# v as the stationary side of the packed values in a fused attention and two-layer-block kernel

## The chip, the core and the metric

The kernel runs on one core of a Trainium2 chip. Its engines are TensorE (PE; its weight loads are shown apart, as PEld), VectorE (DVE), ScalarE (ACT), GpSimd (POOL) and SyncE (SP). The metric is the device time of one execution in microseconds.

## The reference

An attention with 8 batches, 8 heads, 576 positions and head dimension 64 goes through 32 packed queries per head; its output then passes two blocks of matrix products. Cut to what matters here:

```python
def sm_attn(qq, kk, vv):
    s = scale * np.matmul(qq, kk.transpose(0, 1, 3, 2))
    s = s - np.max(s, axis=-1, keepdims=True)
    a = np.exp(s)
    a = a / (np.sum(a, axis=-1, keepdims=True) + 1e-09)
    return np.matmul(a, vv)
p_packed = sm_attn(p, k, v)              # 32 x 64 per head
out = sm_attn(q, p_packed, p_packed)     # 576 x 64 per head
x = out as (4608, 512)
h = ((x @ w1) * (x @ w2)) @ w3 @ w_out
h = g(h @ w_in) @ w_out2                 # g: a piecewise quadratic
```

The change is in the first of the two attentions, in `a / sum` and the product with v.

## The kernel before, in words

The program has three stages: the attention with the first block (to about 546 us), the second block's first product (to about 900 us) and its second. The change lies in the first.

A batch of the first stage is a list of 24 units on PE: 16 `ab_unit`s (L388: two products of 6 matmuls at L398, 128x288 each, multiplied with each other) and then 8 `x2_unit`s (L436: 24 matmuls at L422 through `x2_product`). While the units of batch b run, the attention of batch b+1 is made between them, one step behind a unit: the main loop (L748) puts step `spread[u]` behind unit u. A step has a part for PE and one for the other engines (`ew`); `emit` (L362) issues the first, then the second, and every engine and every DMA queue takes its instructions in the order in which they are issued. The steps of `attention` (L197), for batches 1 to 7 with `joint` set, are:

- `scores_k(G)` (L201), for half G of the heads: 8 matmuls of float32 (L190, through `eight`), DVE's maximum `mx` and `nb`, and ACT's exponential (L217) into a tile `e`, with the row sums into `c["sum"]`. For batch b+2 it stands behind units 20 and 22 of batch b.
- `turn_e(0)` and `turn_e(1)` behind unit 4: 10 transposes of `e` on PE (L234) and ACT's copies into `et` (L242). `turn_e(1)` also makes `rd`, the reciprocal of both halves' sums, on DVE (L248, L249).
- `packed` behind unit 8: 40 matmuls (L260) with `et` as the loaded side (32 columns, one head) and v as the moving side (64 columns); then DVE multiplies with `rd` into `pp` (L268).
- `turn_packed` behind unit 10: PE transposes `pp` (L277), ACT copies the result to `ppt` (L281), and SP loads the next batch's v and pb.
- `scores_q` behind unit 12, `normalise` and `split_a`: the second attention, from `ppt`.
- `build_m` behind units 20 and 22: matmuls of `ppt` with w1 and w2 (L190), split on ACT and DVE at L111 and L112.

Batch 0 and the steps of batch 1 are laid out by hand (`STEPS`, L51, and `TAIL`, L54): b0 and b1 are batch 1's `scores_k`, b4 its `packed`, b5 its `turn_packed`, k0 and k1 batch 2's `scores_k`, y0 to y7 the last `x2_unit`s of batch 0, whose results DVE adds to `xp` (L452), n0 to n3 batch 1's `build_m`, b9 a `normalise`, t1 a `split_a`. The tail ends

```python
'n1', 'n0', 'k0', 'y3', 'b9', 'y4', 'n3', 'n2', 'k1', 'y5', 't1', 'y6', 'y7'
```

In PSUM six banks k0 to k5 go round for the units (`psa`, L96): an `ab_unit` takes two, an `x2_unit` one. A tile of two banks, `psm`, serves the attention steps. Between the units DVE, ACT and the queues also prepare the second block's weights (`weight_tasks`, L628: raw, cvt, cvx, hl), one or two tasks a unit.

Of the kernel before, what the change touches and what calls it, by code (L numbers as in the profile page):

```python
# [8 lines left out]
F32 = mybir.dt.float32  # L9
# [4 lines left out]
AF = mybir.ActivationFunctionType  # L14
# [8 lines left out]
P = 128  # L23
HS = S // 2
NCH = 5
# [37 lines left out]
def fused_kernel(ctx: ExitStack, tc, qT, kT, vv, pb, w1, w2, w3T, wo, win, wout, out):  # L63
# [133 lines left out]
    def attention(b, joint=False):  # L197

        c = {}

        def scores_k(G):  # L201
            def pe():
                heads = loaded["k", b].rearrange("p a (r n) -> p (a r) n", r=2)
                c["ps"] = psm()
                eight([c["ps"][:, r, :HS] for r in range(2)], loaded["p", b][:, G],
                      lambda q: heads[:, 4 * G + q])

            def ew():
                mx = small(1, "mx")
                nc.vector.tensor_reduce(out=mx, in_=c["ps"][:, :, :HS], axis=AX.XY, op=ALU.max)  # L210
                nb = small(1, "nb")
                nc.vector.tensor_scalar(out=nb, in0=mx, scalar1=-SCALE, scalar2=None, op0=ALU.mult)
                if G == 0:
                    c["sum"] = small(2, "sum")
                    c["e"] = []
                e = big()
                nc.scalar.activation(  # L217
                    out=e.rearrange("p (a n) -> p a n", a=2), in_=c["ps"][:, :, :HS], func=AF.Exp,
                    scale=SCALE, bias=nb, accum_out=c["sum"][:, G:G + 1],
                )  # L220
                c["e"].append(e)
                if G == 1:
                    load_q(b)
            return pe, ew

        def turn_e(i):
            def pe():
                if i == 0:
                    c["et"] = a2.tile([CH, 2, NCH, P], F32, name="et", tag="et", bufs=1)
                alone = i and (joint or b == 0)  # L230
                ps = c["turn", i] = psa().rearrange("p (g n) -> p g n", g=2) if alone else psm()
                for G in range(2):
                    for x, ch in enumerate(TURNS[i]):
                        nc.tensor.transpose(  # L234
                            ps[:CHS[ch], G, x * P:(x + 1) * P],
                            c["e"][G][:, ch * CH:ch * CH + CHS[ch]], ident,
                        )

            def ew():
                chs = TURNS[i]  # L240
                rows = min(CHS[ch] for ch in chs)
                nc.scalar.activation(  # L242
                    out=c["et"][:rows, :, chs[0]:chs[-1] + 1, :].rearrange("p g c n -> p g (c n)"),
                    in_=c["turn", i][:rows, :, :len(chs) * P], func=AF.Copy,
                )
                if i == 1:
                    rd = small(2, "rd")
                    nc.vector.tensor_scalar(out=rd, in0=c["sum"], scalar1=1e-9, scalar2=None, op0=ALU.add)  # L248
                    nc.vector.reciprocal(out=rd, in_=rd)  # L249
                    c["rd"] = rd  # L250
            return pe, ew

        def packed():
            def pe():
                c["ps"] = psm()
                for G in range(2):
                    for ch in range(NCH):
                        for q in range(4):
                            h = 2 * q + G
                            nc.tensor.matmul(  # L260
                                c["ps"][32 * q:32 * q + 32, G, :D],
                                c["et"][:CHS[ch], G, ch, 32 * q:32 * q + 32],
                                loaded["v", b][:CHS[ch], ch, h * D:(h + 1) * D],
                                start=(ch == 0), stop=(ch == NCH - 1),
                            )

            def ew():
                nc.vector.tensor_tensor(  # L268
                    out=pp.rearrange("p (r d) -> p r d", r=2), in0=c["ps"][:, :, :D],
                    in1=c["rd"].unsqueeze(2).to_broadcast([P, 2, D]), op=ALU.mult,  # L270
                )
            return pe, ew

        def turn_packed():
            def pe():
                c["ps"] = psm()
                nc.tensor.transpose(c["ps"][:, 0, :P], pp, ident)  # L277

            def ew():
                c["ppt"] = a2.tile([P, P], F32, name="ppt", tag="ppt", bufs=1)  # L280
                nc.scalar.activation(out=c["ppt"], in_=c["ps"][:, 0, :P], func=AF.Copy)  # L281
                if 0 < b < B - 1:
                    load_v(b + 1)
                    load_p(b + 1)
            return pe, ew

        def scores_q(hf):
            def product(x):
                qt = loaded["q", b]
                ps = None if joint and x == 0 else psm()  # L290
                c["ps", x] = [ps[:, r] if ps is not None else psa() for r in range(2)]
                eight([p[:, :HS] for p in c["ps", x]], c["ppt"], lambda q: qt[:, q, x * HS:(x + 1) * HS])

            def pe():
                for x in ((hf,), (0, 1), ())[joint * (1 + hf)]:
                    product(x)

            def ew():
                l = big()
                for r in range(2):  # L300
                    nc.vector.transpose(out=l[:, r * HS:(r + 1) * HS], in_=c["ps", hf][r][:, :HS])
                l3 = l.rearrange("p (c n) -> p c n", n=NP)
                mx = small(S // NP, "qmx")
                nc.vector.tensor_reduce(out=mx, in_=l3, axis=AX.X, op=ALU.max)
                nc.vector.tensor_tensor(
                    out=l3, in0=l3, in1=mx.unsqueeze(2).to_broadcast([P, S // NP, NP]), op=ALU.subtract)
                c["l", hf] = l
                exp = lambda: nc.scalar.activation(out=l, in_=l, func=AF.Exp, scale=SCALE)
                if b:
                    exp()  # L310
                else:
                    later.append(exp)
                if hf == 1 and 0 < b < B - 1:
                    load_k(b + 1)
            return pe, ew

        def normalise(hf):
            def ew():
                l3 = c["l", hf].rearrange("p (c n) -> p c n", n=NP)
                sm = small(S // NP, "qsm")  # L320
                nc.vector.tensor_reduce(out=sm, in_=l3, axis=AX.X, op=ALU.add)
                nc.vector.tensor_scalar(out=sm, in0=sm, scalar1=1e-9, scalar2=None, op0=ALU.add)
                nc.vector.reciprocal(out=sm, in_=sm)
                nc.vector.tensor_tensor(
                    out=l3, in0=l3, in1=sm.unsqueeze(2).to_broadcast([P, S // NP, NP]), op=ALU.mult)
                t = big()
                nc.vector.transpose(out=t, in_=c["l", hf])
                c["t", hf] = t
            return None, ew

        def split_a(hf):
            def ew():
                if hf == 0:
                    at_tile[b] = a1.tile([P, 2, 2, S], F32R, name="at", tag="at", bufs=1)
                at = at_tile[b][:, :, :, hf * HS:(hf + 1) * HS]
                t = c["t", hf].rearrange("p (r n) -> p r n", r=2)
                nc.scalar.activation(out=at[:, :, 0], in_=t, func=AF.Copy)
                nc.vector.tensor_tensor(out=at[:, :, 1], in0=t, in1=at[:, :, 0].bitcast(F32), op=ALU.subtract)
            return None, ew

        def build_m(w, n):
            ps = []

            def pe():
                ps.extend([psa(), psa()])
                eight(ps, c["ppt"], lambda q: w12[w][n][:, q, :])

            def ew():
                m = a1.tile([P, 2, 2, 512], F32R, name=f"m{w}{n}", tag=f"m{w}{n}", bufs=1)
                for G in range(2):  # L350
                    split(m[:, :, G], ps[G])
                m_tile[b, w, n] = m
            return pe, ew

        return (
            [scores_k(0), scores_k(1), turn_e(0), turn_e(1), packed(), turn_packed(),
             scores_q(0), scores_q(1), normalise(0), normalise(1)],
            [split_a(0), split_a(1)],
            {(w, n): build_m(w, n) for w in range(2) for n in range(2)},
        )  # L360
# [931 lines left out]
```

## Time and profile before

| | us |
|---|---|
| median of 3 runs | 1247.66 |
| lowest and highest of them | 1245.33, 1247.72 |
| the profiled execution's own time | 1245.62 |
| its span | 1243.8 |
| PE busy | 1234.9 (99%) |
| DVE busy | 841.6 (68%) |
| ACT busy | 694.9 (56%) |

The span is what the profiler saw from the first to the last instruction. A float32 matmul stands in the trace as two MATMUL and two LDWEIGHTS records; a matmul of the type fp32r and a transpose stand there as one of each. Starts are measured, the ends of PE's records are modelled, so what a stretch costs is read from starts.

### The profile page before, as it was taken

To read this page: it belongs to the slowest core of one execution; us is meant where nothing else is said; L and a number is where in the kernel's file an instruction comes from. 1 tells how busy PE (TensorE), PEld (TensorE's weight loads), DVE (VectorE), ACT (ScalarE), POOL (GpSimd) and SP (SyncE) were. 2 spreads that over 40 slices of the span, in tenths; PEclk is the share of its full clock that TensorE was granted. 3 is DMA by queue.
4 is the path that set the end of the run, shared out by engine and by line. 5 is a ranking of instruction groups with operands and counts; after the bars stand their busy time and mean duration, and the time that the engine had idled before them with its cause. 6 is when DMAs were issued, how large, how long until landed. Compare 5 with 4: busy or idle time off the path is not lost.

```text
span 1243.8 us, 21614 instructions
## 1 busy us (share of the span) xinstructions
PE 1234.9 (99%) x8344; PEld 1100.6 (88%) x8344; DVE 841.6 (68%) x1358; ACT 694.9 (56%) x1184; POOL 47.1 (4%) x86
## 2 busy tenths in 40 slices
PE   8999999999999999999999999999999999999998
PEld 4479899999999899998899999999988999999998
DVE  4765787857777766717797888786777555564645
ACT  6784546453645553526676867776764534444342
POOL 0000100001010101010000000000000000000000
PEclk9999999999999999999999999999999999999999
DMA  9862666555756533179777776869999768586855
GB/s 356 317 248 86 208 227 219 202 176 194 230 173 227 194 126 118 62 267 366 263 256 261 242 271 222 286 216 309 330 395 369 248 236 288 195 284 219 295 193 178
DMA packets 139399, 297.12 MB, mean 239 GB/s; under 512 B 11296, under 2 KB 96736, under 8 KB 135584
## 3 DMA queue, kind: packets, MB, share of 16 engines
q1 hardware_dynamic: 106864, 241.96, 55.9%
q10 hardware_dynamic: 27440, 36.74, 9.0%
q0 software_dynamic: 4992, 17.04, 4.1%
q8 instruction: 65, 1.06, 0.4%
q14 instruction: 38, 0.31, 0.1%
HBM read 195.04 MB, written 100.66 MB: 238 GB/s over the span
## 4 chain that ended last, share of the span: by engine, by line
PE 93%; DMA 4%; DVE 1%; ACT 1%; issue 0%; SPq 0%; ACTq 0%; DVEq 0%
PE psk L398 16%; PE psk L422 16%; PE x L1063 15%; PE x L881 15%; PE z L881 8%; PE z L1063 7%; PE psk L531 4%; PE y L1063 4%; PE y L881 4%; PE psk L190 3%; DMA wi<-wi 2%; PE psm L190 1%; PE psm L260 1%; DMA r<-g 1%; DMA raw<-w3T 1%; PE psm L234 1%
## 5 line engine op out<-in xcount | busy, mean ns | idle before, releaser
L398 PE MATMUL psk<-at,m 128*128 128x288 f32 x1536 | 212.0, 296 | 0.0
L422 PEld LDWEIGHTS psk<-g,w 128*128 128x128 f32 x1536 | 204.3, 188 | 8.2 <-ACT m L111 7.2
L398 PEld LDWEIGHTS psk<-at,m 128*128 128x128 f32 x1536 | 205.1, 188 | 5.4 <-issue 4.2
L422 PE MATMUL psk<-g,w 128*128 128x288 f32 x1536 | 209.6, 296 | 0.0
L881 PE MATMUL x<-x2s,wi 128*128 128x448 f32 (+1 forms) x720 | 161.6, 368 | 0.3 <-DMA wi<-wi 0.3
L881 PEld LDWEIGHTS x<-x2s,wi 128*128 128x128 f32 x720 | 134.4, 188 | 14.7 <-issue 1.0
L1049 DVE TENSOR_TENSOR op<-raw,op 128x896 fp32r<-128x896 f32 (+1 forms) x93 | 100.3, 1114 | 67.4 <-ACT op L1048 67.3
L1048 ACT ACTIVATE op<-raw 128x896 fp32r<-128x896 f32 (+1 forms) x93 | 86.6, 967 | 64.3 <-DVE raw L1035 39.8
L1063 PE MATMUL x<-op,hwi 128*128 128x448 f32 (+1 forms) x480 | 100.5, 368 | 0.3 <-DVE op L1049 0.3
L1063 PEld LDWEIGHTS x<-op,hwi 128*128 128x128 f32 x480 | 89.9, 188 | 9.2 <-DVE op L1049 0.7
L1063 PE MATMUL x<-op,w 128*128 128x448 f32 (+1 forms) x456 | 94.1, 366 | 0.0
L1063 PEld LDWEIGHTS x<-op,w 128*128 128x128 f32 x456 | 85.5, 188 | 7.6
L410 DVE TENSOR_TENSOR tb<-psk,ta 128x288 f32<-128x288 f32 x128 | 57.9, 454 | 49.4 <-PE psk L398 21.5
L892 ACT ACTIVATE r<-r 128x896 f32<-128x896 f32 (+1 forms) x80 | 78.0, 975 | 2.5
L408 ACT ACTIVATE ta<-psk 128x288 f32<-128x288 f32 x128 | 51.7, 407 | 44.5 <-PE psk L398 44.4
L1049 DVE TENSOR_TENSOR op<-r,op 128x896 fp32r<-128x896 f32 (+1 forms) x45 | 48.6, 1108 | 38.7 <-ACT op L1048 38.7
L954 ACT ACTIVATE m<-x 128x448 f32<-128x448 f32 (+1 forms) x40 | 22.2, 555 | 86.6 <-PE x L881 69.1
L895 DVE SCALAR_TENSOR_TENSOR U<-U,r 128x448 f32<-128x448 f32 (+1 forms) x80 | 47.4, 635 | 31.6 <-ACT r L892 31.6
L1048 ACT ACTIVATE op<-r 128x896 fp32r<-128x896 f32 (+1 forms) x45 | 42.1, 961 | 37.3 <-DVE r L1035 18.9
L111 ACT ACTIVATE g<-tb 128x288 fp32r<-128x288 f32 x128 | 56.2, 439 | 8.6 <-DVE tb L410 8.5
L132 ACT ACTIVATE cvt<-raw 128x512 f32<-128x512 f32 (+1 forms) x74 | 48.8, 660 | 20.1 <-DMA raw<-wo 6.2
L531 PE MATMUL psk<-wo,w3f 128*128 128x512 f32 x128 | 57.3, 599 | 2.5 <-DVE w3f L145 2.5
(125 smaller groups left out, 1908.9 us busy)
## 6 DMA issues: line engine op xcount, KB each, us to landing
raw<-g SPq DMA_DIRECT2D x84, 448.0 KB, 4.5
g<-L SPq DMA_DIRECT2D x64, 448.0 KB, 3.6
r<-g SPq DMA_DIRECT2D x44, 448.0 KB, 4.6
g<-U SPq DMA_DIRECT2D x64, 224.0 KB, 4.2
raw<-g SPq DMA_DIRECT2D x24, 512.0 KB, 6.7
ws<-ws SPq DMA_DIRECT2D x42, 256.0 KB, 4.3
v<-vv SPq DMA_DIRECT2D x8, 1280.0 KB, 7.6
wi<-hl ACTq DMA_DIRECT2D x20, 512.0 KB, 4.1
```

What stands on the lines that cost most here:

```text
L111: nc.scalar.activation(out=dst[:, 0], in_=src, func=AF.Copy)
L190: nc.tensor.matmul(ps[r][NP * q:NP * q + NP], stat[64 * r:64 * r + 64, NP * q:NP * q + NP], mov(q)[64 * r:64 * r + 64], start=True, stop=True,
L398: nc.tensor.matmul(ps[w][:, :HS], m_tile[b, w, n][:, s, G, c0 * P:(c0 + 1) * P], at_tile[b][:, G, v, hf * HS:(hf + 1) * HS], start=(k == 0 ...
L408: nc.scalar.activation(out=bs, in_=ps[1][:, :HS], func=AF.Copy)
L410: nc.vector.tensor_tensor(out=g, in0=ps[0][:, :HS], in1=bs, op=ALU.mult)
L422: nc.tensor.matmul(ps, w34[kt][:, s, mt * P:(mt + 1) * P], g_t[kt, hf][:, v, :], start=(kt == kts[0] and n == 0), stop=(kt == kts[-1] and ...
L531: nc.tensor.matmul(acc[4 * hf + m], w3f[hf, j][:, m * P:(m + 1) * P], wof[j], start=(j == 0), stop=(j == 7))
L881: nc.tensor.matmul(bank[s, b][:, :N], w, x2_t[t, q][:, m, k], start=(j == 0 and q in (A11, S1, A12)), stop=(j == 5), skip_group_check=True,)
L892: nc.scalar.activation(out=r, in_=r, func=AF.Square)
L1048: nc.scalar.activation(out=o[:, :, 0], in_=a[0], func=AF.Copy)
L1049: nc.vector.tensor_tensor(out=o[:, :, 1], in0=a[0], in1=o[:, :, 0].bitcast(F32), op=ALU.subtract)
L1063: nc.tensor.matmul(bank[b][d][:, :N], w2_t[q][j // 2][:, 2 * (j % 2) + k, s, d * P:(d + 1) * P], op[x][:, k, v], start=start and k == 0 an ...
```

## The change

For batches 1 to 7 (`joint`), each half's sums get their reciprocal in `scores_k`, and ACT scales `e` in place. In `packed`, v is the loaded side (64 columns) and `et` the moving one (32 columns); the two heads of a pair write partitions 0 to 63 and 64 to 127 of one tile, which ACT copies to `ppt`. DVE's product, PE's transpose and the step `turn_packed` go (an empty step stays in its place), and the loads of v and pb are issued behind `packed`. The lines after L221 move down by 6 to 31.

```diff
@@ scores_k, ew
                 c["e"].append(e)
+                if joint:
+                    rd = small(1, "rd")
+                    nc.vector.tensor_scalar(
+                        out=rd, in0=c["sum"][:, G:G + 1], scalar1=1e-9, scalar2=None, op0=ALU.add)
+                    nc.vector.reciprocal(out=rd, in_=rd)
+                    nc.scalar.activation(out=e, in_=e, func=AF.Copy, scale=rd)
                 if G == 1:
                     load_q(b)
@@ turn_e, ew
-                if i == 1:
+                if i == 1 and not joint:
@@ packed
+            def turned():
+                ps = c["ps"] = psm()
+                for q in range(4):
+                    for ch in range(NCH):
+                        for G in range(2):
+                            h = 2 * q + G
+                            nc.tensor.matmul(
+                                ps[D * G:D * G + D, 0, 32 * q:32 * q + 32],
+                                loaded["v", b][:CHS[ch], ch, h * D:(h + 1) * D],
+                                c["et"][:CHS[ch], G, ch, 32 * q:32 * q + 32],
+                                start=(ch == 0), stop=(ch == NCH - 1),
+                            )
+
+            def copy():
+                c["ppt"] = a2.tile([P, P], F32, name="ppt", tag="ppt", bufs=1)
+                nc.scalar.activation(out=c["ppt"], in_=c["ps"][:, 0, :P], func=AF.Copy)
+                if 0 < b < B - 1:
+                    load_v(b + 1)
+                    load_p(b + 1)
+            if joint:
+                return turned, copy
@@ turn_packed
+            if joint:
+                return None, lambda: None
```

Two places in the order of the instructions. The first is PE in batch 1, where batch 2's packed values are made (`psk` are the units' banks, `at` and `m` their operands, `pp` the scaled packed values). Before:

```order
L260 MATMUL psm<-v,et 32x64 x40
L398 MATMUL psk_1864<-at,m_1402 128x288 x6
L398 MATMUL psk_1871<-at,m_1417 128x288 x6
L398 MATMUL psk_1886<-at,m_1402 128x288 x6
L398 MATMUL psk_1893<-at,m_1417 128x288 x6
L277 MATMUL psm<-ident,pp 128x128
L398 MATMUL psk_1919<-at,m_1402 128x288 x6
```

And now:

```order
L266 MATMUL psm<-et,v 64x32 x40
L429 MATMUL psk_1876<-at,m_1404 128x288 x6
L429 MATMUL psk_1883<-at,m_1419 128x288 x6
L429 MATMUL psk_1898<-at,m_1404 128x288 x6
L429 MATMUL psk_1905<-at,m_1419 128x288 x6
L429 MATMUL psk_1923<-at,m_1404 128x288 x6
```

The 40 matmuls stand at the same place with their sides exchanged, and the transpose two units later is gone.

The second is DVE at the end of the tail, from k1's maximum on (`xp` are the additions of y5 to y7, `at` belongs to t1, `tb` to the first units of batch 1; the number behind psk is the bank). Before:

```order
L210 TENSOR_REDUCE mx_1514<-psm_1505 128x1
L212 TENSOR_SCALAR nb_1516<-mx_1514 128x1
L452 TENSOR_TENSOR xp11_1082<-psk3_1522,xp11_1082 128x288
L338 TENSOR_TENSOR at_1359<-big_1458,at_1359 128x2x288
L452 TENSOR_TENSOR xp21_1126<-psk4_1539,xp21_1126 128x288
L452 TENSOR_TENSOR xp31_1209<-psk5_1554,xp31_1209 128x288
L410 TENSOR_TENSOR tb_1595<-psk1_1586,ta_1593 128x288
```

And now:

```order
L210 TENSOR_REDUCE mx_1520<-psm_1511 128x1
L212 TENSOR_SCALAR nb_1522<-mx_1520 128x1
L224 TENSOR_SCALAR rd_1526<-sum_1437 128x1
L226 RECIPROCAL rd_1526<-rd_1526 128x1
L483 TENSOR_TENSOR xp11_1092<-psk3_1532,xp11_1092 128x288
L369 TENSOR_TENSOR at_1361<-big_1464,at_1361 128x2x288
L483 TENSOR_TENSOR xp21_1128<-psk4_1549,xp21_1128 128x288
L483 TENSOR_TENSOR xp31_1211<-psk5_1564,xp31_1211 128x288
L441 TENSOR_TENSOR tb_1605<-psk1_1596,ta_1603 128x288
```

The reciprocal of the sums, which ACT's exponential makes, now stands between `nb` and the evacuations of the banks.

## Rows read from the trace of the kernel before

**Rows 1.** The page, part 1: engine, busy us (share of the span), instructions.

```profile
PE 1234.9 (99%) x8344; PEld 1100.6 (88%) x8344; DVE 841.6 (68%) x1358; ACT 694.9 (56%) x1184; POOL 47.1 (4%) x86
```

**Rows 2.** Stretches: us, busy time and instructions by engine, granted clock, DMA.

```profile
core 0: us, PE busy (x) PEld busy (x) DVE busy (x) ACT busy (x) POOL busy (x), PEclk, DMA share, GB/s
66.00:330.00 264.00, 263.50 (x2620) 238.00 (x2619) 189.95 (x393) 142.55 (x323) 17.51 (x32) 1.00 0.57 194
```

**Rows 3.** Chain of waits, 197 to 258 us: start us, us, what.

```profile
212.81 1.26 PE psm L260 x80
...
217.47 0.11 PE psm L277
```

**Rows 4.** Line 260: durations in ns, min/median/max, first and last start.

```profile
L260 PEld LDWEIGHTS psm<-v,et x640: 106/110/113, 36.7 to 453.5; 116*32 116x32 f32 x128, 112*32 112x32 f32 x32
L260 PE MATMUL psm<-v,et x640: 217/219/243, 36.7 to 453.5; 116*32 116x64 f32 x128, 112*32 112x64 f32 x32
```

**Rows 5.** Timeline of PE, 212.7 to 214.02 us: start us, us, line and operation.

```profile
212.74 1.33 PE L260 MATMUL psm<-v,et 116*32 116x64 f32 x80
214.00 0.40 PE L398 MATMUL psk<-at,m 128*128 128x288 f32 x1
```

**Rows 6.** Line 398, as in rows 4.

```profile
L398 PE MATMUL psk<-at,m x1536: 289/294/697, 72.4 to 521.3; 128*128 128x288 f32 x192
```

**Rows 7.** Chain of waits over the span, the piece at 33.30 us.

```profile
33.30 3.44 PE psk L531 x8
```

**Rows 8.** Timeline of PE's weight loads, 5.0 to 6.6 us.

```profile
4.91 1.75 PEld L572 LDWEIGHTS psm<-ident 128*128 128x128 f32 x15
```

**Rows 9.** Line 572, as in rows 4.

```profile
L572 PEld LDWEIGHTS psm<-ident x32: 192/272/333, 1.4 to 6.5; 128*128 128x128 f32 x32
```

**Rows 10.** Timeline of DVE, 127 to 140 us: k0, y3, y4, k1, y6 and y7.

```profile
129.18 0.15 DVE L212 TENSOR_SCALAR nb<-mx 128x1 f32<-128x1 f32 x1
129.38 0.46 DVE L452 TENSOR_TENSOR xp<-psk,xp 128x288 f32<-128x288 f32 x1
...
132.54 0.42 DVE L452 TENSOR_TENSOR xp<-psk,xp 128x288 f32<-128x288 f32 x1
...
136.05 0.15 DVE L212 TENSOR_SCALAR nb<-mx 128x1 f32<-128x1 f32 x1
...
138.43 0.82 DVE L452 TENSOR_TENSOR xp<-psk,xp 128x288 f32<-128x288 f32 x2
```

**Rows 11.** Timeline of ACT, 129 to 139 us: k0's exponential and t1's copy.

```profile
129.43 0.74 ACT L217 ACTIVATE big<-psm,nb 128x576 f32<-128x576 f32 x1 [1.99 <-DVE nb L212]
130.07 0.19 ACT L217 ACTIVATION_READ_ACCUMULATOR big<-psm,nb 128x1 f32 x1
...
137.05 0.67 ACT L337 ACTIVATE at<-big 128x576 fp32r<-128x576 f32 x1
```

**Rows 12.** Chain of waits, 130 to 148 us: y5 to y7, first units of batch 1.

```profile
132.35 4.96 PE psk L422 x36
137.31 7.90 PE psk L398 x60
```

**Rows 13.** Lines 248, 249 and 308, as in rows 4.

```profile
L248 DVE TENSOR_SCALAR rd<-sum x8: 158/162/165, 32.3 to 445.9; 128x2 f32<-128x2 f32 x8
L249 DVE RECIPROCAL rd<-rd x8: 165/166/168, 32.5 to 446.1; 128x2 f32<-128x2 f32 x8
L308 ACT ACTIVATE big<-big x16: 683/686/687, 48.4 to 470.5; 128x576 f32<-128x576 f32 x16
```

**Rows 14.** Timeline of ACT, 256.5 to 260 us, behind a `scores_k(1)`.

```profile
257.57 0.40 ACT L454 ACTIVATE st<-psk 128x288 f32<-128x288 f32 x1
258.23 0.41 ACT L408 ACTIVATE ta<-psk 128x288 f32<-128x288 f32 x1 [0.25 <-PE psk L398]
259.81 0.41 ACT L408 ACTIVATE ta<-psk 128x288 f32<-128x288 f32 x1 [1.17 <-PE psk L398]
```

**Rows 15.** Timeline of ACT, 212.6 to 217.6 us, behind a `packed`.

```profile
215.10 0.41 ACT L408 ACTIVATE ta<-psk 128x288 f32<-128x288 f32 x1 [1.67 <-PE psk L398]
```

**Rows 16.** Timelines of SP's queue and of ACT, 318 to 362 us.

```profile
319.86 10.32 SPq L118 DMA_DIRECT2D raw<-win  x4
...
361.77 0.66 ACT L132 ACTIVATE cvt<-raw 128x512 f32<-128x512 f32 x1
```

## Prediction

> **What bounds the kernel now.** I read the page first: PE is busy for 1234.9 of 1243.8 us [rows 1]. Then the stretches: from 66 to 330 us, where batches 0 to 3 or so run, PE is busy 263.5 of 264.0 us at a granted clock of 1.00, DVE 190 us and ACT 143 us [rows 2]. So in the attention stage the end is set by how long TensorE's stream takes, and other engines matter only where they are late with a PSUM bank. Then the chain of waits over one batch: it is PE alone, and the two steps that the change touches on PE stand there with 1.26 us (`packed`, L260) and 0.11 us (transposing its result, L277) [rows 3].
>
> **How `packed` runs today.** 40 matmuls appear as 80 records, so each float32 matmul is two passes with a weight load each. One batch's stretch lasts 1.33 us [rows 5]; less the 0.219 us of its last record [rows 4], the starts span 1.11 us. Four heads write four 32-column strips of the array side by side, so these are 20 steps of four, and 19 intervals: **58 ns a step**. What limits a step? The moving side: `w34` work of 512 float32 columns takes 3.44 us for 8 passes [rows 7], 430 ns a pass, 0.84 ns a column; 64 columns make 54 ns, 32 make 27. The rest of the step is 4 ns. The weight load: where it stands uncovered, at the first matmul after another shape, that matmul is recorded longer by it. L260's first lasts 243 against 219 ns [rows 4]: 24 ns for 32 columns. The L398 matmul right behind L260 lasts 0.40 us against a median of 294 ns [rows 5, 6]: about 105 ns for 128 columns. A straight line between the two gives **51 ns for 64 columns**. Today 24 ns of load hide under 54 ns of move: together they would be 78, and the step is 58.
>
> **The change on PE, batches 1 to 7.** v (64 columns a head) becomes the loaded side and 32 columns move. Still 40 matmuls, 80 passes, but only two strips of 64 columns stand side by side, so 40 steps of two instead of 20 of four. Per step the load is 51, the move 27. Do they overlap when the load is the longer? The 16 warm-up matmuls load and move 128 float32 columns each: 15 of their loads span 1.75 us [rows 8], less the last one's 192 ns [rows 9] 14 intervals of 111 ns, where the load is 105 and the move 108. Overlap holds up to equality, with 3 to 6 ns on top of the longer one. For the new step that makes 55 to 58 ns; I take **56**. The ends if that is wrong: 31 ns, were the load hidden (27+4), and 82, were it not overlapped at all (51+27+4). So:
> - `packed`: 39 x 56 = 2.18 us against 1.11, +1.07 us. The moved columns halve and the loaded ones double; the longer one decides, and it has changed sides.
> - The first load is uncovered with 51 in place of 24 ns: +0.03.
> - The transpose goes: -0.11 [rows 3].
> Together +0.99 us a batch, seven batches: **+6.9 us**, all on the path, since PE has no idle time there to take it in.
>
> **The change on ACT and DVE.** Gone per batch from DVE: the product pp and two small steps on two columns. Added per half G, twice a batch: an add and a reciprocal on one column (0.16 and 0.17 us, priced by the two-column rows, [rows 13]) and on ACT a scaled copy of 128x576, for which L308's 0.69 us [rows 13] is the nearest row. That is 1.4 us a batch of ACT, which has idle time; as busy time I cost it at nothing. The wait counts: DVE's add now needs ACT's finished sum, and queues in order. At batch 2's first half, `nb` ends at 129.33; the exponential starts at 129.43 and its sum is read at 130.26 [rows 10, 11]. Today DVE goes on at 129.38. After it stands until 130.3, works 0.35, and goes on at about 130.7: **1.3 us of DVE held** each time. ACT is held 0.4 us and works 0.69: 1.1 us.
>
> Who waits behind? In steady batches the next DVE item is weight preparation, on which PE does not wait; and ACT's next items are a staging copy at 257.57 and `ta` at 258.23, PE's next at 259.81 [rows 14], so ACT is back in step one unit later. A bank is asked for again three units (4.7 us, 36 matmuls of 132 ns, [rows 12]) after its use. I cost these at 0. In the tail of batch 0 it is different: right behind DVE's wait stand evacuations of PSUM. `y4`'s, at 132.54 [rows 10], starts 1.3 us later, at 133.85, and frees its bank at 134.3; `y6` asks for it at 132.35+1.65 = 134.0 [rows 12]: 0.3 us late. The second half adds 1.3 on DVE, and on ACT `at` (137.05, [rows 11]) goes behind the scaled copy to about 139.4; DVE's half of `at` ends at 140.85, and `y6`'s evacuation, at 138.43 today [rows 10], is over at 141.3. The bank's next user is the third unit of batch 1, at 137.31+3.17+0.3 = 140.8 [rows 12]: 0.5 late. Sum **+0.9 us**, once; bounds 0 and the two holds in full, 2.6.
>
> The rest: the copy `ppt` comes two units earlier, in a gap where ACT idles 1.67 us before `ta` [rows 15], with a weight copy behind it that PE does not need: 0. On SP one weight load moves behind v and pb, which wait for `packed`'s end: it was issued with the group that ends at 330.2, and its conversion on ACT comes at 361.77 [rows 16], so 5 us of delay cost nothing.
>
> **Sum.** 6.9 + 0.9 = +7.8 us. On the profiled execution's 1245.62 us that is 1253.4; the median of the three runs, 1247.66, lies 2.0 us higher and gives 1255.5. The runs stand at two levels, so I name **1255.0 us**, nearer the median.
>
> **Rivals.**
> - **The load hides (not slower).** If a 64-column load took at most the 27 ns of the move, `packed` would take 39 x 31 = 1.21 us, +0.10, and with the first load and the transpose's 0.11 the seven batches come out at about 0; with the 0.9 us that is +1.0 and 1246.6 to 1248.7 us. It decides at 0.42 ns a loaded column. Against: the two uncovered loads give 0.75 and 0.82 ns a column. For: both are readings of modelled ends, and the loads that the trace shows for transposes are not on this line. Chance 0.09.
> The Trainium skill (TensorEngine Tiling (Array Packing), Instruction Overhead) speaks against this case: a matmul with hardly any moving columns takes as long as one with 60, and tiling should not be taken from a dimension that is already small. By it the 32-column step would cost what today's 64-column step does, 58 ns, and the sum would be +8.4 in place of +7.8 us; no matmul of this trace moves fewer than 64 columns, so no row shows it.
> - **Load and move stop overlapping.** In one strip, the next load would wait until the move is through: 82 ns a step, 3.20 us, +2.01 us a batch, +14.1 and +0.9: 1260.6 to 1262.7 us. Against: today's 58 is under the 78 of both. For: no row has a load longer than its move. Chance 0.06.
> The Trainium skill (TensorE: Matmul & The Clock Gate, Part 3, The mechanism) says that a load overlaps with running matmuls only where the row groups differ, and here all loads use the same rows. By that rule this rival is the forecast; today's step of 58 ns disagrees with it.
> - **The two strips load one after the other.** 80 loads of 51 with 4 between: 4.35 us, +3.16 a batch, 1268.6 to 1270.7 us. Against: today four loads of 24, 96 ns, fit into a step of 58. Chance 0.02.
> - **The holds reach PE in every batch.** 14 holds of 1.3 us, 18 us: up to 1272. It decides where a bank is freed later than the three units that six banks give; the rows leave 2 us and more outside the tail. Parts of it are likelier than the whole. Chance 0.03.
>
> **How the numbers follow.** The forecast has 0.80. Its own range: lowest run 1245.33 with 55 ns a step and no hold, 1245.33+6.6 = 1251.9; highest 1247.72 with 58 ns and both holds in full, 1247.72+7.5+2.6 = 1257.8. With a part of the holds elsewhere the range is 1251.5 to 1260, which leaves out the hidden load, the rivals above 1260 and little else. A difference of 0.2%, 2.5 us, is about what a measurement of this kernel can tell from none. Slower by more: the forecast and the three dear rivals, 0.89; within: nearly all of the hidden load, 0.09; faster: 0.02, were the holds free too and the runs on the lower level.
>
> **What would show it.** Right: the new matmuls' stretch in one batch at about 2.4 us from first start to last end, starts in twos 56 ns apart; PE still busy all through the stage and its rows elsewhere unchanged; one short PE wait each on DVE near 134 and 141 us; later stages shifted by 7 to 8 us and otherwise alike. Wrong: a stretch near 1.4 us (load hidden) or 3.4 us (no overlap); PE waits on ACT or DVE near the `k` steps of steady batches; or a shift that PE's records do not carry.

## The result, and the profile after

| | before | after |
|---|---|---|
| median, us (runs) | 1245.57 (5) | 1256.48 (5) |
| lowest and highest | 1244.93, 1247.72 | 1255.59, 1261.7 |

The ratio is 1.0088, with an interval of 1.0076 to 1.0101: the change costs 10.9 us. The profiled execution took 1261.7 us and is the slowest of its five, for a reason that comes at the end of this section. The changed kernel was therefore profiled once more (`again` below: 1256.9 us, span 1255.1), and where nothing else is said, "after" is that profile.

Part 1 of its page, which answers to [rows 1]:

```profile
PE 1243.5 (99%) x8337; PEld 1108.6 (88%) x8337; DVE 842.0 (67%) x1365; ACT 704.0 (56%) x1198; POOL 46.9 (4%) x86
```

The span grew by 11.3 us, PE's busy time by 8.6: most of the loss is more work on PE, the rest PE standing still. The standing is in the attention stage; the stretch of [rows 2], where PE was idle for 0.5 us, now has 2.7:

```profile
66.00:330.00 264.00, 261.28 (x2556) 235.06 (x2555) 185.11 (x385) 143.44 (x321) 17.45 (x32) 1.00 0.55 188
```

The new work is in the chain of waits over two batches (start us, us, what), which answers to [rows 3]:

```profile
218.24 2.46 PE psm L266 x80
220.70 6.60 PE psk L429 x48
...
279.26 2.46 PE psm L266 x80
```

`packed` takes 2.46 us in place of 1.26, and the 48 unit matmuls behind it run on without the transpose. From one `packed` to the next it is 61.02 us. The line itself, which answers to [rows 4], and the new scaling of `e`:

```profile
L266 PEld LDWEIGHTS psm<-et,v x560: 132/138/139, 99.5 to 464.5; 116*64 116x64 f32 x150, 112*64 112x64 f32 x37
L266 PE MATMUL psm<-et,v x560: 222/223/243, 99.5 to 464.6; 116*64 116x32 f32 x150, 112*64 112x32 f32 x37
L227 ACT ACTIVATE big<-big,rd x14: 775/778/780, 84.3 to 447.7; 128x576 f32<-128x576 f32 x14
```

The moved columns fell from 64 to 32, the loaded ones rose from 32 to 64. The starts come in twos; the 80 of a batch span 2302 ns, the first step 79 of them, the other 38 **58.3 ns** each. Before, the 80 spanned 1114 ns, with a first step of 80 and **56.3 ns** in each of the other 18; the prediction's 58 had spread the longer first step over all 19.

The other part of the loss lies in front of the steady batches. PE's waits from 88 to 160 us (us in total, times, longest); before, this view has no row at all for that stretch:

```profile
PE psk L429 <- ACT ta L439: 1.5, 1, 1.5
PE psk L429 <- DVE xp L483: 0.5, 1, 0.5
PE psk L453 <- DVE xp L483: 0.2, 1, 0.2
```

The two waits on `xp` are at 136 and 143 us. The long one ends at 151.41, and the chain of waits says what is late (SPq is SP's queue):

```profile
145.98 0.03 SPq L118
146.01 0.04 issue
146.05 4.25 DMA raw<-win
150.30 0.02 issue
...
150.38 0.13 ACT cvt L132
150.51 0.44 issue
150.95 0.41 ACT ta L439
...
151.41 5.82 PE psk L429 x42
```

A load of raw weights, issued at 146.05, lands so late that its conversion `cvt` holds ACT, with PE's `ta` behind it. Why is it issued so late? Its tile lies where `xp` lay, and in the program it waits for the stores of `xp`. POOL's timeline has these stores, first before, then after:

```profile
139.18 1.07 POOL L456 DMA_DIRECT2D x2d<-xp  x2 [1.77 <-DVE xp L452]
```

```profile
143.30 1.07 POOL L487 DMA_DIRECT2D x2d<-xp  x2 [1.71 <-DVE xp L483]
```

The last of them land 2.1 us after issue, at 141.8 and 145.9 us, and SP issues the load at 141.92 and 146.05. ACT's timelines have what follows, again before and after:

```profile
146.02 0.69 ACT L132 ACTIVATE cvt<-raw 128x512 f32<-128x512 f32 x1 [3.97 <-DMA raw<-win]
```

```profile
150.38 0.67 ACT L132 ACTIVATE cvt<-raw 128x512 f32<-128x512 f32 x1 [4.67 <-DMA raw<-win]
```

Before, ACT waited there too, for 4 us, and was done just in time for PE. After, it is 4.4 us later, while PE has 2.9 us of delay of its own by then; the other 1.5 it stands.

Set against each other, PE's matching unit matmuls move by these amounts: +0.5 us at 92 us, +1.2 at batch 1's `packed` and -0.1 at its transpose, +0.4 at 134, +0.8 at 140, +1.5 at 147, then +1.10 in each of the six further batches, and +0.4 net at the borders of the later stages. The sum, 11.3, is the span's difference. (By starts PE loses more at 134 and 140 us than the 0.2 and 0.5 of the view above, whose waits begin at modelled ends of matmuls.) Of the 0.5 at 92 us the line of the scaling tells whose it is:

```profile
  PEld psm L240: 0.3, 1
```

That row stands under "who waited for it" in the answer for L227: the transposes of batch 1's `e` now wait for the scaled `e`.

**The first profile's own extra.** There PE also stands for 3 us at 172.8 us, because ACT waits for a store of prepared weights (ACT, then PE):

```profile
174.94 0.63 ACT L713 ACTIVATE hl<-cvx 128x512 fp32r<-128x512 f32 x1 [4.29 <-DMA ws<-hl]
...
175.92 6.33 PE L453 MATMUL psk<-g,w 128*128 128x288 f32 x34 [3.13 <-ACT ta L439]
```

The store was issued at 160.13 and took 14.8 us. Behind this wait PE runs at a lower clock for a while (columns as in [rows 2]):

```profile
175.90:178.00 2.10, 2.08 (x10) 2.08 (x11) 2.10 (x6) 1.05 (x3) 0.00 (x0) 0.62 0.06 20
```

By PE's starts the wait costs 3.3 us and the clock behind it another 1.7. In the profile of `again` PE does not stand there. This is not a cost that the change brings every time.

### The profile page after: what moved, and what is told of

It reads as the page before. It is cut to its first block, busy times and chain, and to the rows that moved or that the text cites. A ratio compares the mean times of both kernels' runs of the same rounds, so it can differ in the third digit from the quotient of the medians.

```text
span 1259.9 us, 21622 instructions
## 1 busy us (share of the span) xinstructions
PE 1245.9 (99%) x8337; PEld 1110.8 (88%) x8337; DVE 842.1 (67%) x1365; ACT 704.1 (56%) x1198; POOL 46.9 (4%) x86
## 4 chain that ended last, share of the span: by engine, by line
PE 90%; DMA 5%; DVE 2%; ACT 1%; issue 1%; SPq 0%; ACTq 0%; DVEq 0%
PE psk L453 15%; PE x L1094 15%; PE x L912 15%; PE psk L429 14%; PE z L912 7%; PE z L1094 7%; PE psk L562 4%; PE y L1094 4%; PE y L912 4%; PE psk L190 2%; DMA wi<-wi 2%; PE psm L266 1%; DMA ws<-hl 1%; PE psm L190 1%; DMA raw<-w3T 1%; DMA r<-g 1%
## 5 line engine op out<-in xcount | busy, mean ns | idle before, releaser
L1080 DVE TENSOR_TENSOR op<-raw,op 128x896 fp32r<-128x896 f32 (+1 forms) x93 | 100.3, 1114 | 68.0 <-ACT op L1079 67.8
```

The source lines that it names most:

```text
L1080: nc.vector.tensor_tensor(out=o[:, :, 1], in0=a[0], in1=o[:, :, 0].bitcast(F32), op=ALU.subtract)
```

## The experiments

**again**: the changed kernel as it is.

> The changed kernel once more, for a second profile. Load theory (a step of the packed product is as long as its 64-column load, and the rest is DVE's wait for the sums in the tail): about 1256.5 us, 11 above the kernel before; the packed product takes 2.46 us a batch with starts in twos 58 ns apart, steady batches 61.0 us against 59.9, PE waits of 0.3, 0.7 and 1.5 us between 134 and 155 us. The wait of 3.1 us near 176 us, behind a store of weights, comes from the DMA's own spread and need not return. Rival (that wait belongs to the change): it returns in the same size.

Measured: 1256.67 us (1255.8 to 1259.02) against 1246.37, ratio 1.0085 (1.007 to 1.01). The wait of 3 us did not come back, the rest did.

**e1_scale_only**: the scaling of `e` alone, `packed` with the old sides, a plain copy on DVE where the product was, and the transpose.

```diff
 # scores_k as in the changed kernel; packed and turn_packed as before, but for
+                if joint:
+                    nc.vector.tensor_scalar(
+                        out=pp.rearrange("p (r d) -> p r d", r=2), in0=c["ps"][:, :, :D],
+                        scalar1=1.0, scalar2=None, op0=ALU.mult)
+                    return
```

> The scaling of e stays where the change puts it, but the packed product has its old sides, with the transpose, and DVE copies instead of multiplying. Load theory: the packed product is back at 1.26 us and the steady batches at 59.9 us, while the tail keeps its waits of about 0.4, 0.3, 0.7 and 1.5 us: 1245.6 + 2.9 = 1248.5 us. Rival (the waits for the sums cost in every batch, and the sides little): steady batches above 60.5 us and 1253 or more. Rival (the scaling costs nothing at all): 1245.6.

Measured: 1249.95 us (1248.46 to 1251.51), ratio 1.0025 (1.0015 to 1.0036): +3.6 by the medians. Its chain of waits:

```profile
218.15 1.26 PE psm L286 x80
219.41 3.40 PE psk L429 x24
222.80 0.11 PE psm L308
...
278.09 1.26 PE psm L286 x80
```

59.94 us from one `packed` to the next: in steady batches the added work on ACT and DVE costs nothing. PE's waits from 88 to 160 us are those of the changed kernel:

```profile
PE psk L429 <- ACT ta L439: 1.4, 1, 1.4
PE psk L429 <- DVE xp L483: 0.6, 1, 0.6
```

By starts, PE loses 0.45, 0.44, 0.82 and 1.39 us at the four places: 3.1 in all, where 0.9 were forecast.

**e2_swap_only**: the sides exchanged alone.

```diff
                 c["e"].append(e)
-                if joint:
...
-                    nc.scalar.activation(out=e, in_=e, func=AF.Copy, scale=rd)
```

> The sides are exchanged, but e is not scaled and the packed values stay without their division by the row sums (this part of the computation is left out); the reciprocal is made where it was before and not used. Load theory: steady batches 61.0 us, no new waits in the tail, seven times 1.1 us: 1253.3 us. Rival (the scaling carries the loss): 1246 to 1249.

Measured: 1254.65 us (1254.06 to 1256.5), ratio 1.0068 (1.0053 to 1.0083). The chain has `packed` with its 2.46 us, +1.10 a batch, and of the waits in front of the steady batches 0.2 us is left:

```profile
217.59 2.46 PE psm L260 x80
220.04 6.60 PE psk L423 x48
```

By PE's starts the two parts add up: 3.1 us for the scaling, 7 x 1.10 for the sides. By the medians they are 3.6 and 8.3 us, 10.3 for both at once, with intervals of 1.3 to 1.9 us to either side of each.

**e3_late_scale**: the changed kernel with reciprocal and scaling as a step of their own, behind unit 1 of the batch before (in the tail, batch 1's behind u7).

```diff
+        def scale_e():
+            def ew():
+                for G in range(2):
...
+                    nc.scalar.activation(out=c["e"][G], in_=c["e"][G], func=AF.Copy, scale=rd)
+            return None, ew
-TAIL = ['u7', 'x0',
+TAIL = ['u7', 'e1', 'x0',
...
+            spread[1] = sc
```

> The changed kernel with the reciprocals and the scaling of e in a step of their own, behind unit 1 of the batch before (for batch 1 behind u7), so that DVE never waits for an exponential that has just been issued. Load theory: the waits in the tail go, steady batches stay at 61.0 us: 1253.3 to 1253.8 us, 3 us under the changed kernel. Rival (the tail's waits come from the longer product itself): no gain, 1256.5.

Measured: 1255.75 us (1255.15 to 1257.55), ratio 1.0077 (1.0062 to 1.0092): a miss. The waits at 134 and 140 are gone and the one behind the raw load is down to 0.6, but batch 1's scaling is now later than its transposes need it (ACT, then PE):

```profile
91.17 1.44 ACT L260 ACTIVATE big<-big,rd 128x576 f32<-128x576 f32 x2 [1.51 <-DVE rd L257]
```

```profile
92.00 1.32 PE L234 MATMUL psm<-ident,big 128*116 128x128 f32 x8 [1.55 <-ACT big L260]
```

PE loses 2.0 us there in place of 0.5. The edit cured one place and spoiled another, and the expectation had looked at the first alone.

**e5_late_batch2** mends that: only batch 2's scaling is moved (`if joint and b != 2` in `scores_k`, `scale_e` behind unit 1 of batch 1).

> The changed kernel, but batch 2's reciprocal and scaling, which stand in the tail of batch 0 in front of the evacuations, come as a step of their own behind the first unit pair of batch 1. All other batches as changed. My theory: the waits on DVE at 134 and 140 us go, the late raw transfer's wait at 147 us falls from 1.5 to 0.6 us or less, batch 1's own wait at 92 us (0.5) stays: 2 us less than the changed kernel, 1254.6. Rival, the held engines of the tail cost nothing and the 3 us outside the steady batches come from elsewhere: 1256.5.

Measured: 1255.59 us (1253.72 to 1256.13), ratio 1.0071 (1.0056 to 1.0087), 1 us over the value named. In its profile the waits at 134 and 140 us are gone and the one at 147 is down from 1.5 us to 0.3, all by this one move; what is left from 88 to 160 us is

```profile
PE psk L441 <- ACT ta L451: 0.3, 1, 0.3
```

This profile has a wait of 1.1 us at 75 us that no other has, ahead of everything that was edited; it is a wait of this execution. What the move is worth is read from PE's starts (2.4 us of 2.8 at the three places); the median, which lies 1.1 us under that of `again`, is too coarse to tell 2 from 1.

**e4_four_strips**: v loaded in four strips of 32 columns.

```diff
-                        for G in range(2):
+                        for r in range(4):
+                            G, x = divmod(r, 2)
...
-                                ps[D * G:D * G + D, 0, 32 * q:32 * q + 32],
-                                loaded["v", b][:CHS[ch], ch, h * D:(h + 1) * D],
+                                ps[32 * r:32 * r + 32, 0, 32 * q:32 * q + 32],
+                                loaded["v", b][:CHS[ch], ch, h * D + 32 * x:h * D + 32 * x + 32],
```

> The changed kernel, but each head's v is loaded as two strips of 32 columns side by side: 80 matmuls a batch instead of 40, four strips at once. My theory (a step lasts as long as the longer of load and move, plus 4.8 ns, and in the changed kernel that is the load of 64 columns): load 24, move 27, so a step of 32 ns, a stretch of about 1.4 to 1.5 us instead of 2.46, steady batches 59.9 us long again, the tail's waits (about 3 us) kept: 1249.5 us. Rival 1, a step is as long as 64 moving columns however few move: steps stay 58 ns, stretch 2.46, 1256.5. Rival 2, the number of passes sets the pace, so much time for each record whatever its shape (29 ns for each of today's 80): 160 passes, stretch 4.7 us, about 1272. Rival 3, strips move one after the other (27 + 27 and 4 is 58 too): a step of 112, stretch 4.5 us, about 1271.

Measured: 1264.57 us (1261.88 to 1265.99), ratio 1.0145 (1.0131 to 1.0159): slower than the changed kernel, and no expectation had it. Where PE's stream flows, the stretch is as my theory has it, at 225 us for instance 160 starts within 1.37 us, some 34 ns a step. But in three of the seven batches PE then stands with nothing to wait for. Timeline of PE and stretches (columns as in [rows 2]) around 347 us:

```profile
345.35 1.55 PE L267 MATMUL psm<-et,v 116*32 116x32 f32 x159
349.44 0.21 PE L267 MATMUL psm<-et,v 112*32 112x32 f32 x1 [2.54 <-issue]
```

```profile
347.00:349.00 2.00, 0.00 (x0) 0.00 (x0) 0.00 (x0) 0.00 (x0) 0.00 (x0) 1.00 0.00 0
349.00:350.00 1.00, 0.56 (x3) 0.42 (x3) 0.00 (x0) 0.28 (x1) 0.00 (x0) 0.68 0.00 0
350.00:352.00 2.00, 2.00 (x10) 2.00 (x10) 0.69 (x1) 1.20 (x3) 0.00 (x0) 0.50 0.60 157
...
353.00:356.00 3.00, 3.00 (x24) 3.00 (x24) 2.77 (x6) 2.01 (x5) 0.00 (x0) 1.00 0.91 253
```

One pass of 160 is missing when the engine stops; DVE and ACT stand too; and then the granted clock is 0.50, the 1.2 GHz level, for some 3 us. One transfer moves in the meantime, from 346.99 to 348.00: in the DMA queues of 346.9 to 348.1 us

```profile
q8 instruction: 1, 0.02, 5.3%
```

The instruction queue brings 16 KB, and PE goes on 1.44 us after it has landed. In the batches without a wait, no such transfer falls into the stretch. In batch 2 PE stands only when all 160 passes are through, in front of an ordinary unit matmul, which starts at 165.47 us after 3.61 us of idle time, put down to "issue" like the others. By PE's starts the three waits cost nearly 13 us, with the lower clock behind each, of the 20.4 by which this span is longer than before.

**e7_half_load**: the changed kernel with 32 of 64 columns of v loaded.

```diff
-                                ps[D * G:D * G + D, 0, 32 * q:32 * q + 32],
-                                loaded["v", b][:CHS[ch], ch, h * D:(h + 1) * D],
+                                ps[D * G:D * G + 32, 0, 32 * q:32 * q + 32],
+                                loaded["v", b][:CHS[ch], ch, h * D:h * D + 32],
```

> The changed kernel, but only the first 32 of the 64 columns of each head's v are loaded (half of the packed values is not computed: the other half is a copy of the first), everything else of packed as changed: 40 matmuls, two strips, 32 moving columns. One size alone differs, the loaded columns. My theory: a step of 32 ns in place of 58, a stretch of about 1.45 us. The rivals that leave the load out (as long as 64 moving columns; a fixed time a pass; strips moved one after the other): 58 ns and 2.46 us as in the changed kernel. The time itself is little worth, three small copies a batch are added on ACT: some 1249 to 1250 us by my theory, 1256.5 by the others.

Measured: 1249.03 us in one run. The chain of waits has

```profile
215.06 1.39 PE psm L266 x80
216.45 6.60 PE psk L432 x48
```

1265 ns from first to last start, 53 in the first step and **31.7** in each of the other 38. Passes, moved columns and strips are those of the changed kernel; the loaded columns alone are halved, and the step falls from 58.3 to 31.7. These 27 ns for 32 loaded columns are 0.83 ns a column; it is at least that, since at 32 columns the move of 27 ns may be the longer side.

**e6_four_late2**: four strips, late scaling, batch 1 with the old sides (`if b > 1` in `packed` and `turn_packed`).

> The best of the parts: four strips of 32 loaded columns, scaling as a step of its own behind unit 1, and batch 1 left with the old sides so that nothing of it stands in the tail. By my theory PE's packed costs what it cost before (four strips, 32 ns a step of twice as many) and the transpose's 0.11 us goes, six times, with a rest of the late raw transfer of 0 to 0.6 us: 1245.5 to 1247, the same as the kernel before within 0.1%. If four strips gain nothing (rivals of e4_four_strips): 1253 or more.

Measured: 1255.64 us (1252.68 to 1257.41), ratio 1.0074 (1.006 to 1.0087): a miss, and for e4's reason in its profile, which is of the fastest of the five runs. PE stands in two batches of six; PE's timeline, and the DMA queues from 275.4 to 276.4 us:

```profile
273.11 1.50 PE L271 MATMUL psm<-et,v 116*32 116x32 f32 x152
277.82 0.27 PE L271 MATMUL psm<-et,v 112*32 112x32 f32 x8 [3.21 <-issue]
```

```profile
q8 instruction: 1, 0.02, 5.5%
```

That transfer landed at 276.36, PE went on 1.46 us later. Where nothing stops it, this version takes 60.05 us a batch, 0.13 more than the kernel before, where 0.1 less was expected.

**e8_four_halves**: e6 with its 80 matmuls in two groups of 40.

```diff
-            def turned():
-                ps = c["ps"] = psm()
-                for q in range(4):
+            def turned(i):
+                if i == 0:
+                    c["ps"] = psm()
+                ps = c["ps"]
+                for q in (2 * i, 2 * i + 1):
...
-                return turned, copy
+                c["half"] = lambda: turned(1), copy
+                return lambda: turned(0), lambda: None
```

> e6_four_late2, but packed's 80 matmuls stand in two groups of 40, behind unit 8 and behind unit 10 (where the empty step was). In the profiles of e4_four_strips and e6_four_late2 the stretch of four strips has the length forecast (1.49 us), but in 3 of 7 and 2 of 6 batches PE stands for 1.3 to 4 us within it or behind it with nothing that it waits for, each time until 1.4 to 1.5 us after one of the 16-KB transfers of the instruction queue. My theory: the 160 passes use up more instructions at once than lie ready, and 40 matmuls at a time don't (the kernel before sends 40 at a time and never stands). Then no such wait is left, and PE has 39 steps of 33 ns and one more uncovered load against 19 of 58, less the transpose: +0.1 us a batch, with a rest of the late raw transfer 1246.4 to 1248.0 us. Rival, four strips of 32 columns stall by themselves (the strips' data, or the psum tile): the waits stay in some batches, 1251 us or more.

Measured: 1250.51 us (1249.86 to 1250.6), ratio 1.0035 (1.0021 to 1.0049). The long waits are gone and with them the spread (0.7 us, against 4.7 in e6). One short wait is left in 12 groups:

```profile
278.47 0.63 PE L273 MATMUL psm<-et,v 116*32 116x32 f32 x48
279.37 0.46 PE L273 MATMUL psm<-et,v 116*32 116x32 f32 x32 [0.27 <-issue]
```

It too ends 1.34 us after an instruction transfer has landed; in two other groups such a transfer runs and PE does not stand. The theory of the instructions' supply fits better than the rival, in a weaker form: smaller groups make the wait rare and short, they don't exclude it. No run has the same passes with the instructions already there, so the rival is not excluded by this one alone. The time was missed by 2.5 us because I had priced the second group's border too low. The chain of waits:

```profile
213.90 0.83 PE psm L273 x58
214.72 3.40 PE psk L438 x24
218.12 0.83 PE psm L273 x58
218.95 3.40 PE psk L438 x24
```

2 x 0.83 us stand against 1.26 + 0.11 before, and the first units behind each group are some 0.2 us longer than otherwise (3.40 against 3.17 to 3.19 for 24), once more than before: +0.5 us a batch, 3 us in all. No version of the changed sides beat the kernel before.

## Why the prediction was right or wrong

**Right: the side and the mechanism.** A step costs what the longer of load and move costs, plus some 5 ns with two strips (before, with four, 2.5 over a move of 54; in e4, also with four, 7 over 27). e7 and e2 show it, each with one thing changed: the load alone carries the step, and the swap alone carries the 1.10 us a batch. Load plus move less a fixed 22 ns would fit 58.3 and 31.7 as well, and miss 56.3 by 2; the warm-up matmuls speak against it, whose steps of 111 ns with 128 columns on each side [rows 8, 9] would be some 190.

**Mis-sized: "for the new step that makes 55 to 58 ns; I take 56".** Measured 58.3, the upper end. The starts of a batch's `packed` span 1.19 us more than before, where 1.10 were forecast (1.07 and the first load's 0.03), the transpose gives back 0.1, and seven batches come to 7.7 in place of 6.9. The load is 0.83 ns a column, 53 ns for 64, where the line through two uncovered loads said 51; the rest of a step is 5 ns.

**Wrong: "Sum +0.9 us, once".** The part that was worked out came nearly as said: the two banks of y6 and of batch 1's third unit are late by 0.4 and 0.8 us (0.3 and 0.5 forecast, which make 0.8 and not 0.9). Two waits are missing in the sum. The late evacuations of the tail were followed into their PSUM banks alone; the other consumer of `xp` is the store, and for the last store, y7's, a raw load waits on SP, and for that load ACT, and behind ACT's conversion `ta`, and for `ta` PE: 1.5 us, the largest of the four. And batch 1's own scaling at 90 us was nowhere costed; the text speaks of steady batches and of the tail: 0.5 us. Together 3.2 in place of 0.9 (3.1 in e1), also above the bound of 2.6, which counted DVE's holds and not what they make late elsewhere. e1 has these waits without the swap, e2 has 0.2 us of them without the scaling, and e5 loses two of them and most of a third by moving one step.

**The scaled copy on ACT** took 0.78 us, not the 0.69 of L308. Holds of ACT grew by a tenth of a microsecond.

**Costed at 0 and 0 it was:** the work on ACT and DVE in steady batches (e1: 59.94 us), and the earlier `ppt` copy.

**The sum** of +7.8 us should have been +10.9. That 1255.0 lies only 1.5 below the result owes something to luck: it was set near the median of the three runs then known, 1247.66, and with two more of the same kernel the median is 1245.57. On that, the sum would have said 1253.4, 3.1 too low.

**The rivals.** The hidden load would show steps of 31 ns, the two loads one after the other 4.35 us a batch; neither is there. Without overlap the step were 82 ns. It is 58.3, with a load of some 53 and a move of 27: they do overlap. The Trainium skill (TensorE: Matmul & The Clock Gate, Part 3, The mechanism) lets a load overlap where row groups differ, or where it goes to the background buffer; all loads here use the same rows, so what is seen is the second case or none of the rule's. The Trainium skill (TensorEngine Tiling (Array Packing), Instruction Overhead) has a matmul with one moving column cost as much as one with 60, which, as the prediction read it, would give 58 ns here, the very number measured; e7 tells the two apart, with 32 moving columns at 31.7 ns a step, so no floor at 60 float32 columns is there. That the holds reach PE in every batch is excluded by e1.

## What to carry to other kernels

Before the sides of a matmul are exchanged, price both: loaded and moved columns cost the same here (0.83 and 0.84 ns a float32 column and pass), they overlap, and the larger one decides; strips side by side work at the same time (two of 64 loaded columns in steps of 58 ns, four of 32 in steps of 34), so what counts is how many steps there are and the longer side of one. What was saved on the way out, a transpose of 0.11 us and work on engines that had time, was never on the path or hardly so. And when an evacuation gets later, follow every consumer of its result, the store and whoever waits for its memory too, not only the bank it frees: the wait that cost most came out two queues and an engine further on.

## What the runs showed of the hardware that was not expected

**Instructions may run out.** 160 passes in 1.4 us, against 80 in 1.1 us before, seem to outrun the supply: in 3 of 7 batches of e4, 2 of 6 of e6, PE stood for 1.3 to some 3.6 us and went on 1.4 to 1.5 us after a 16-KB transfer of the instruction queue had landed, five times of five. Over the span this queue has

```profile
q8 instruction: 70, 1.15, 0.4%
```

transfers in e4 and 65 before. The Trainium skill (Runtime: NRT & Kernel Launch, Instruction fetch mechanics) says that instructions come in blocks of 16 KiB and that crossing a border is mostly hidden; the first agrees with these transfers, and the second holds for the kernel before, whose 80 passes of the same kind never stood (a transfer from 213.37 to 214.30 us lies in one of its stretches), but not for 160 in a row, if it is the supply. That it is the supply is inferred from the times of the transfers, from e8 and from e4's batch 2, where the pass that comes late is none of the strips'; the trace does not name the wait.

**A wait can cost twice.** Behind a wait PE can come back at the 1.2 GHz level: in e4 all three times, after standing 2.0, 3.6 and 2.5 us, around 350 us at a granted clock of 0.50, for some 3 us, worth another 1.3 us; and in the first profile of the changed kernel, after 3.1 us, worth 1.7. In e6, after standing 3.2 us at 275 us, it did not (granted 1.00 on either side); why not is open.

**The start varies by 2 us.** In the profiles of e1 and e2 PE waits 2.1 and 2.0 us for `w3f` near 13 us, and runs the next 3 us at a lower clock; before, it waits there too, 1.6 us at the longest, and runs on at a granted clock of 1.00. In e1's stretches

```profile
13.00:15.00 2.00, 1.37 (x2) 0.64 (x3) 1.27 (x2) 1.94 (x4) 0.00 (x0) 0.73 1.03 420
15.00:18.00 3.00, 3.00 (x5) 1.21 (x4) 1.39 (x2) 2.90 (x5) 0.00 (x0) 0.61 1.06 420
```

with all 16 DMA engines busy. e1 has the same instructions there as the kernel before. It may be a part of the spread of some 2 to 3 us among the runs of one kernel (e1's own lie from 1248.5 to 1251.5); it was seen in two profiles and not tested.
